# Rounding a weight block from the upper word's digits while the lower word is still being added

## The chip, the cores and the metric

The kernel runs on one core of a Trainium2 chip. The time is the device time of one execution in microseconds (us), and the figure quoted for a kernel is the median of its runs. Beside the runs there is one profiled execution, whose trace gives the start, the duration and the waits of every instruction on the engines: PE (matrix products) with PEld (its weight loads), DVE (vector), ACT (scalar), POOL (GpSimd) and SP (which issues DMAs).

## The reference, cut to what matters

Attention in hash buckets over q, k and v (2 batches, 8 heads, 768 positions, 64 wide) gives x with 1536 rows of 512. Two dense layers follow, the first with a gate, the second with a leaky slope:

```python
g = x @ w_gate
silu = g * (1.0 / (1.0 + np.exp(-g)))
x = silu * (x @ w_val) @ w_out            # d_ff 1536
h = x @ w_in
g = np.maximum(h, 0.0) + alpha * np.minimum(h, 0.0)
return g @ w_out                          # d_ff 2048
```

The attention's inputs are float32. The weights reach the chip as 64-bit floating-point numbers, in blocks of 128 x 512, and are turned into float32 there.

## The kernel before, in words

**Precision.** PE takes operands in a shortened float32 form. Every operand is therefore a pair: a high half `h`, which is the number rounded to that form, and a low half `l`, which is the number less `h`. `mm3` (line 608) multiplies a weight pair by an activation pair in three matmuls, in this order: high by high (line 611), high by low (612), low by high (613). So the third matmul of each group is the first that needs the low half.

**Order of the work.** The attention is one long row of steps (`attention`), which computes scores, takes the greatest of each row, subtracts, takes the exponential and multiplies by v. The first dense layer works on groups of 256 rows of x: `stage1(g)` for g = 0 to 3 as soon as the attention has finished that group's rows, with further attention steps between its own (`RATES` says how many), and `stage1w` on 512 columns for the rest. `stage2` is the second layer, three times 512 columns. The order in which the instructions stand on each engine within `stage1` is set by a scheduler that works from the dependencies and its own estimates; a few instructions are pinned to the order in which they are written (`pin`), among them those of `w_early` and of all of `stage1w` and `stage2`. Each engine then works off its row in order, and an instruction that waits holds up all that stand behind it.

**A new weight block.** The first layer has 36 blocks. Each is made once, while `stage1(0)` uses it; the pair is then written to memory (`w_put`) and later groups load it from there. The second layer's 32 blocks are made by `w_early` (12, during groups 2 and 3) and `w_late` (20, during `stage1w`). A block of 64-bit numbers arrives in `raw64` (two buffers). `round64` makes float32 of it, in integers:

1. ACT, line 509: the lower word, scaled, gives in `wr` the digits that the upper word lacks, rounded.
2. DVE, lines 510 and 512: shifts and masks of the upper word give sign, exponent and leading digits in `wt`.
3. POOL, line 514: the integer sum of the two, written over `wt`.

Then the pair is made in `wb`:

4. ACT, line 549 (`w_h`): `wt` rounded, the high half.
5. POOL or DVE in turn, line 556 (`w_l`): `wt` less the high half, the low half. Of the 36 blocks of the first layer POOL does the even ones and DVE the odd ones (`PL`).

`w_ahead` runs these steps a few blocks ahead of the block in use (`LEAD`). `wt` has three buffers, `wr` two, `wb` five; `WB` holds the first and the last of these.

Of the kernel before, what the change touches and what calls it, by code (L numbers as in the profile page):

```python
# [8 lines left out]
F32 = mybir.dt.float32  # L9
F32R = mybir.dt.float32r  # L10
I32 = mybir.dt.int32
U32 = mybir.dt.uint32
AF = mybir.ActivationFunctionType
ALU = mybir.AluOpType
# [9 lines left out]
WB = (3, 5)  # L24
# [22 lines left out]
def lsh_attention_moe_kernel(  # L47
# [12 lines left out]
    nc = tc.nc  # L60
# [4 lines left out]
    P = 128  # L65
# [15 lines left out]
    def f32(ap):  # L81
        return ap.bitcast(F32)
# [390 lines left out]
    NWT = len(seq)  # L473
    fresh = [w not in seq[:i] for i, w in enumerate(seq)]
    new = [n or w >= F2I for n, w in zip(fresh, seq)]
    raw, wt, ready = {}, {}, {}
    ws = Bag()
    ws.pin = True
    ws.load = ws.conv = ws.h = ws.l = ws.used = ws.put = 0
# [5 lines left out]
    def pin(ins):  # L485

        if ws.pin:
            tc.keep_in_program_order(ins)

    def raw_load(w):  # L490
        t = wp.tile([P, 512, 2], I32, tag="raw64", name="raw64", bufs=RAWB)
        pin(nc.sync.dma_start(out=t, in_=wblk[w].bitcast(I32).rearrange("p (f t) -> p f t", t=2)))
        return t
# [9 lines left out]
        elif w < F2I:  # L503
            nc.sync.dma_start(out=f32(w_tile(i)), in_=scratch[w])

    def round64(t, a):

        r = wp.tile([P, 512], I32, tag="wr", name="wr", bufs=2)
        pin(nc.scalar.activation(out=r, in_=t.bitcast(U32)[:, :, 0], func=AF.Copy, scale=float(2.0 ** -29)))
        pin(nc.vector.tensor_scalar(out=a, in0=t[:, :, 1], scalar1=3, scalar2=0x3FFFFFF8,  # L510
                                    op0=ALU.logical_shift_left, op1=ALU.bitwise_and))
        nc.vector.scalar_tensor_tensor(out=a, in0=t[:, :, 1], scalar=-0x40000000, in1=a,  # L512
                                       op0=ALU.bitwise_and, op1=ALU.bitwise_or)
        pin(nc.gpsimd.tensor_tensor(out=a, in0=a, in1=r, op=ALU.add))  # L514

    def w_conv(i):
        w = seq[i]
        if w >= F2I:
            wt[i] = fin.w[:, w - F2I, :]
        elif fresh[i]:  # L520
            wt[i] = wp.tile([P, 512], F32, tag="wt", name="wt", bufs=WB[0])
        if i in raw:
            round64(raw.pop(i), wt[i].bitcast(I32))

    def w_late():

        rs = []
        for w in late + [None] * RAWB:
            if len(rs) == RAWB or w is None:
                r, v = rs.pop(0)  # L530
                round64(r, fin.w[:, v - F2I, :].bitcast(I32))
            if w is not None:
                rs.append((raw_load(w), w))
            yield

    def w_early():

        for w in early:
            r = raw_load(w)
            yield  # L540
            t = wp.tile([P, 512], F32, tag="wt", name="wt", bufs=WB[0])
            round64(r, t.bitcast(I32))
            yield
            nc.sync.dma_start(out=whole[w - F2I], in_=t)
            yield
# [5 lines left out]
    def w_l(i):  # L551

        if new[i]:
            n, m = PL
            eng = nc.gpsimd if i % n < m else nc.vector
            eng.tensor_tensor(out=ready[i][:, 1, :], in0=wt.pop(i), in1=f32(ready[i])[:, 0, :], op=ALU.subtract)  # L556

    def w_put(i):
        if fresh[i] and seq[i] < F2I:
# [8 lines left out]
    def w_ahead(n):  # L568

        for name, k, fn in (("load", 2, w_load), ("conv", 1, w_conv), ("h", 0, w_h)):  # L570
            upto(name, n + LEAD[0] + k, fn)
        upto("l", n + LEAD[0], w_l)
        upto("h", n + LEAD[1], w_h)
        upto("put", n + 1, w_put)
        upto("conv", n + LEAD[2], w_conv)
        while ws.load < min(NWT, n + (LEAD[3] if fresh[min(ws.load, NWT - 1)] else LEAD[2])):
            upto("load", ws.load + 1, w_load)
# [176 lines left out]
    wp = ctx.enter_context(tc.tile_pool(name="wp", bufs=1))  # L754
# [27 lines left out]
    def prime(k):  # L782

        if k == 60:
            setup_alpha()
        k -= PRIME[0]
        if k >= 0 and k % PRIME[1] == 0:
            i = k // PRIME[1]
            upto("load", min(i, 7), w_load)
            if i >= 4:  # L790
                upto("conv", min(i - 3, 4), w_conv)
# [7 lines left out]
    at.alone = False  # L799
    at.tag = dict(S="SSM", m="S", hp="S", po="po")  # L800
    early_steps = w_early()
    ws.pin = False
    for g, rate in enumerate(RATES):
# [77 lines left out]
```

## Time and profile before

| | us |
|---|---|
| median of 3 runs (912.88 to 914.37) | 914.33 |
| the profiled execution | 911.48 |
| its span, first to last instruction | 909.7 |
| PE busy in the span | 840.9 (92%) |
| DVE busy | 576.1 (63%) |
| ACT busy | 440.4 (48%) |
| POOL busy | 378.2 (42%) |
| mean granted clock of PE, as a share of the full one | 0.981 |

A busy share is a mean over stages with different limits, so the stages are read one by one. Up to about 60 us the attention runs alone; from there to about 240 us the first layer's blocks are made and used; from about 240 to 560 us groups 1 to 3 run beside the rest of the attention; then `stage1w`, and from about 640 us `stage2`. "Busy" includes time in which an instruction has begun and is held up by something other than a semaphore.

### The profile page before, as it was taken

How to read it: one execution, taken by the hardware profiler on the slowest of the kernel's cores; microseconds unless marked ns; L12 is line 12 of the kernel's file. 1: busy time of each engine (PE TensorE's matmuls, PEld its weight loads, DVE VectorE, ACT ScalarE, POOL GpSimd, SP SyncE). 2: the span in 40 equal slices, each digit the busy share in tenths (PEclk: the TensorE clock that was granted, in tenths of full speed). 3: DMA queues.
4: the chain of work that ended last, by engine and by line, in shares of the span. 5: the costliest groups of instructions: out<-in, count | busy, mean ns of one | idle time of the engine just before them, and what ended most of it. 6: DMA issues, size and time to landing. Idle time of an engine off the chain costs nothing.

```text
span 909.7 us, 13016 instructions
## 1 busy us (share of the span) xinstructions
PE 840.9 (92%) x4816; PEld 734.1 (81%) x4816; DVE 576.1 (63%) x856; ACT 440.4 (48%) x760; POOL 378.2 (42%) x327
## 2 busy tenths in 40 slices
PE   4797788777899999999999999999999999999998
PEld 3576677666798999999999987788888888888886
DVE  5599999988766657677777537663543353435432
ACT  5687566646555565656565323222433343333331
POOL 4214665766533212232222225543444445435442
PEclk8899989999999999999999999999999999999999
DMA  9424676979999756767766698887200010001001
GB/s 219 102 76 160 215 255 220 261 223 268 306 323 293 218 177 232 250 217 229 261 204 219 219 342 295 331 334 267 105 1 1 1 48 0 1 9 39 1 0 47
DMA packets 63487, 158.45 MB, mean 174 GB/s; under 512 B 18112, under 2 KB 24256, under 8 KB 63424
## 3 DMA queue, kind: packets, MB, share of 16 engines
q1 hardware_dynamic: 61264, 152.07, 50.7%
q0 software_dynamic: 2016, 5.51, 2.9%
q8 instruction: 38, 0.62, 0.3%
q14 instruction: 25, 0.20, 0.1%
q10 hardware_dynamic: 144, 0.05, 0.0%
HBM read 132.44 MB, written 25.17 MB: 173 GB/s over the span
## 4 chain that ended last, share of the span: by engine, by line
PE 68%; DVE 14%; POOL 3%; ACT 3%; DMA 3%; issue 2%; SPq 0%; POOLq 0%; DVEq 0%; ACTq 0%
PE po L319 8%; PE gp L611 6%; PE gp L613 5%; PE gp L612 5%; PE op L618 5%; PE hp L613 5%; PE op L617 5%; PE hp L612 5%; PE hp L611 5%; PE op L616 5%; PE yp L613 3%; PE yp L611 3%; PE yp L612 3%; DVE wt L510 2%; DMA wb<-w 2%
## 5 line engine op out<-in xcount | busy, mean ns | idle before, releaser
L606 POOL TENSOR_TENSOR gl<-ex,gh 128x512 fp32r<-128x512 f32 (+1 forms) x108 | 118.3, 1095 | 213.4 <-ACT gh L603 157.7
L611 PE MATMUL gp<-xh,wb 128*128 128x256 f32 (+1 forms) x480 | 156.4, 326 | 10.5 <-ACT wb L549 5.4
L613 PE MATMUL gp<-xh,wb 128*128 128x256 f32 (+1 forms) x480 | 151.1, 315 | 9.7 <-POOL wb L556 6.6
L612 PE MATMUL gp<-xl,wb 128*128 128x256 f32 (+1 forms) x480 | 149.5, 312 | 2.6 <-POOL xl L348 2.6
L319 PE MATMUL po<-se,vv 128*128 128x256 f32 x576 | 143.2, 385 | 9.1 <-DVE xf L341 3.4
L319 PEld LDWEIGHTS po<-se,vv 128*128 128x128 f32 x576 | 103.8, 193 | 22.3 <-ACT se L312 5.0
L549 ACT ACTIVATE wb<-w 128x512 fp32r<-128x512 f32 x96 | 60.7, 632 | 117.8 <-PE hp L613 79.1
L611 PEld LDWEIGHTS gp<-xh,wb 128*128 128x128 f32 x480 | 93.9, 196 | 21.0 <-ACT wb L549 9.0
L603 ACT ACTIVATE gh<-ex 128x512 fp32r<-128x512 f32 (+1 forms) x108 | 57.8, 535 | 105.2 <-DVE ex L600 46.7
L556 POOL TENSOR_TENSOR wb<-w,wb 128x512 fp32r<-128x512 f32 x48 | 62.1, 1294 | 110.3 <-ACT wb L549 106.2
L613 PEld LDWEIGHTS gp<-xh,wb 128*128 128x128 f32 x480 | 94.4, 197 | 15.8 <-POOL wb L556 7.6
L612 PEld LDWEIGHTS gp<-xl,wb 128*128 128x128 f32 x480 | 94.3, 196 | 7.0 <-POOL xl L348 2.8
L312 ACT ACTIVATE se<-se 128x1536 f32<-128x1536 f32 x48 | 71.3, 1485 | 50.5 <-DVE se L307 50.3
L556 DVE TENSOR_TENSOR wb<-w,wb 128x512 fp32r<-128x512 f32 x48 | 36.4, 758 | 91.2 <-ACT wb L549 91.2
L307 DVE SCALAR_TENSOR_TENSOR se<-se,mb 128x1536 f32<-128x1536 f32 x48 | 83.7, 1744 | 8.3 <-PE mb L302 8.0
L282 ACT ACTIVATE se<-S 128x512 f32<-128x512 f32 x144 | 80.1, 593 | 16.9 <-PE S L281 15.6
L514 POOL TENSOR_TENSOR wt<-wt,wr 128x512 int32<-128x512 int32 x48 | 68.2, 1421 | 47.3 <-DVE wt L512 33.7
L280 PE MATMUL S<-QA,kt 128*128 128x256 f32 x288 | 80.3, 308 | 1.6 <-ACT se L282 1.4
L611 PE MATMUL yp<-gh,wb 128*128 128x256 f32 (+1 forms) x240 | 76.2, 319 | 5.4 <-ACT wb L549 3.8
L613 PE MATMUL yp<-gh,wb 128*128 128x256 f32 (+1 forms) x240 | 72.9, 310 | 6.4 <-POOL wb L556 4.3
L281 PE MATMUL S<-qb,kt 76*128 76x256 f32 x288 | 73.5, 286 | 1.4 <-ACT kt L203 1.2
L611 PE MATMUL hp<-xh,wb 128*128 128x512 f32 x192 | 74.7, 389 | 0.0
(94 smaller groups left out, 1848.4 us busy)
## 6 DMA issues: line engine op xcount, KB each, us to landing
wb<-w SPq DMA_DIRECT2D x144, 512.0 KB, 4.4
raw<-in_wblk_dram SPq DMA_DIRECT2D x68, 512.0 KB, 4.3
w<-wb SPq DMA_DIRECT2D x36, 512.0 KB, 5.0
qr<-in_q_dram SPq DMA_DIRECT2D x24, 256.0 KB, 3.7
kt<-in_k_dram POOLq DMA_DIRECT2D x14, 384.0 KB, 8.1
nat<-in_k_dram SPq DMA_DIRECT2D x8, 384.0 KB, 5.2
vv<-in_v_dram SPq DMA_DIRECT2D x16, 192.0 KB, 6.8
whole<-wt SPq DMA_DIRECT2D x12, 256.0 KB, 2.2
```

The costliest lines, as they stand in the source:

```text
L280: nc.tensor.matmul(pt[:, i, :], lhsT=ka[:, sl], rhs=qa, start=True, stop=False)
L281: nc.tensor.matmul(pt[:, i, :], lhsT=kb[:, sl], rhs=qb, start=False, stop=True)
L282: nc.scalar.activation(out=u.se[:, 2 * j:2 * j + 2, :], in_=pt, func=AF.Copy)
L307: nc.vector.scalar_tensor_tensor(out=u.se, in0=u.se, scalar=FLOOR, in1=u.mx[:, None, :].to_broadcast([P, NC, GQ]), op0=ALU.max, op1=ALU.su ...
L312: nc.scalar.activation(out=u.se, in_=u.se, func=AF.Exp, scale=SCALE)
L319: nc.tensor.matmul(it.po[:, u.x, :], lhsT=VV[it.b, it.p][:, kb, u.x * D:u.x * D + P], rhs=u.se[:, kb, :], start=kb == 0, stop=kb == NC - 1)
L514: pin(nc.gpsimd.tensor_tensor(out=a, in0=a, in1=r, op=ALU.add))
L556: eng.tensor_tensor(out=ready[i][:, 1, :], in0=wt.pop(i), in1=f32(ready[i])[:, 0, :], op=ALU.subtract)
L606: nc.gpsimd.tensor_tensor(out=l, in0=ex, in1=f32(h), op=ALU.subtract)
L611: nc.tensor.matmul(pt, lhsT=h, rhs=ah, start=first, stop=False)
L612: nc.tensor.matmul(pt, lhsT=h, rhs=al_, start=False, stop=False)
L613: nc.tensor.matmul(pt, lhsT=l, rhs=ah, start=False, stop=last)
```

## The change

The POOL addition of a first-layer block (line 514) writes its sum into `wr`, and no longer over `wt`. `wt` keeps the upper word's digits alone. The high half (step 4) is the rounding of those digits, so that it needs DVE's line 512 and no longer POOL's line 514. The low half (step 5) is the sum, from `wr`, less the high half; so the pair still adds up to the same number. Step 5 now waits for the addition and for the rounding, which may run side by side. `wr` gets three buffers and `wt` two. The blocks of the second layer are made as before, with the new buffer counts.

```diff
-    def round64(t, a):
+    def round64(t, a, apart=False):
...
-        r = wp.tile([P, 512], I32, tag="wr", name="wr", bufs=2)
+        r = wp.tile([P, 512], I32, tag="wr", name="wr", bufs=WB[0])
...
-        pin(nc.gpsimd.tensor_tensor(out=a, in0=a, in1=r, op=ALU.add))
+        if apart:
+            pin(nc.gpsimd.tensor_tensor(out=r, in0=a, in1=r, op=ALU.add))
+        else:
+            pin(nc.gpsimd.tensor_tensor(out=a, in0=a, in1=r, op=ALU.add))
+        return r
...
-            wt[i] = wp.tile([P, 512], F32, tag="wt", name="wt", bufs=WB[0])
+            wt[i] = wp.tile([P, 512], F32, tag="wt", name="wt", bufs=2)
         if i in raw:
-            round64(raw.pop(i), wt[i].bitcast(I32))
+            whl[i] = round64(raw.pop(i), wt[i].bitcast(I32), apart=True).bitcast(F32)
...
-            t = wp.tile([P, 512], F32, tag="wt", name="wt", bufs=WB[0])
+            t = wp.tile([P, 512], F32, tag="wt", name="wt", bufs=2)
...
-            eng.tensor_tensor(out=ready[i][:, 1, :], in0=wt.pop(i), in1=f32(ready[i])[:, 0, :], op=ALU.subtract)
+            w = wt.pop(i)
+            w = whl.pop(i) if i in whl else w
+            eng.tensor_tensor(out=ready[i][:, 1, :], in0=w, in1=f32(ready[i])[:, 0, :], op=ALU.subtract)
```

In the changed kernel the addition of line 514 is line 515 for these blocks, line 549 is 553, and from line 556, which is 562, all numbers are six higher.

The dependencies being others, the scheduler also sets the instructions in another order, from the first blocks of `stage1(0)` to the end of the attention. Two places on DVE show it. In the names, the number behind a tile tells one block's buffer from another's; a block's `wr` has the number after its `wt`. The first place is the last block but two of `stage1(0)`, `wt_2080`, whose subtraction gives `wb_2111`. Before:

```order
L510 TENSOR_SCALAR wt_2080<-raw64_1994 128x512
L594 SCALAR_TENSOR_TENSOR ex_2132<-ex_2132,gp_2088 128x256
L512 SCALAR_TENSOR_TENSOR wt_2080<-raw64_1994,wt_2080 128x512
L297 TENSOR_REDUCE mq_2350<-mt_2347 128x2
L307 SCALAR_TENSOR_TENSOR se_2016<-se_2016,mb_2369 128x1536
L510 TENSOR_SCALAR wt_2114<-raw64_2039 128x512
L556 TENSOR_TENSOR wb_2111<-wt_2080,wb_2111 128x512
```

Now:

```order
L510 TENSOR_SCALAR wt_2080<-raw64_1994 128x512
L600 SCALAR_TENSOR_TENSOR ex_2132<-ex_2132,gp_2088 128x256
L512 SCALAR_TENSOR_TENSOR wt_2080<-raw64_1994,wt_2080 128x512
L562 TENSOR_TENSOR wb_2111<-wr_2081,wb_2111 128x512
L286 TENSOR_TENSOR m2_2472<-se_2296 128x512
```

Three instructions stood between the block's line 512 and its subtraction; now none does. Over the 18 blocks that DVE subtracts, 77 rows stood between the two, and 64 do now.

The second place is the last block of `stage1(0)`, `wt_2160`, whose subtraction gives `wb_2194`. Before:

```order
L335 STREAM_TRANSPOSE xf_2407<-den_2404 128x256
L289 TENSOR_TENSOR m1_2475<-m2_2472 128x256
L510 TENSOR_SCALAR wt_2160<-raw64_2086 128x512
L336 RECIPROCAL r8_2408<-xf_2407 128x8
L512 SCALAR_TENSOR_TENSOR wt_2160<-raw64_2086,wt_2160 128x512
L337 STREAM_TRANSPOSE den_2404<-r8_2408 128x256
L341 TENSOR_TENSOR xf_2407<-po_2254,den_2404 64x256 x2
L286 TENSOR_TENSOR m2_2586<-se_2416 128x512
L556 TENSOR_TENSOR wb_2194<-wt_2160,wb_2194 128x512
```

Now:

```order
L289 TENSOR_TENSOR m1_2475<-m2_2472 128x256
L510 TENSOR_SCALAR wt_2160<-raw64_2086 128x512
L512 SCALAR_TENSOR_TENSOR wt_2160<-raw64_2086,wt_2160 128x512
L307 SCALAR_TENSOR_TENSOR se_2016<-se_2016,mb_2369 128x1536
L562 TENSOR_TENSOR wb_2194<-wr_2161,wb_2194 128x512
L335 STREAM_TRANSPOSE xf_2407<-den_2404 128x256
L336 RECIPROCAL r8_2408<-xf_2407 128x8
L337 STREAM_TRANSPOSE den_2404<-r8_2408 128x256
L341 TENSOR_TENSOR xf_2407<-po_2254,den_2404 64x256 x2
```

The attention's output step (lines 335 to 341) and one line 286 stood ahead of the last subtraction and now stand behind it; all else that DVE did up to that point it still does up to that point.

## Rows read from the trace of the kernel before

**Rows 1.** Busy time by stretch: the stretch, its length, each engine's busy us
```profile
76.00:242.00 166.00, 128.80 (x796) 111.52 (x795) 156.47 (x213) 101.18 (x181) 106.46 (x86) 0.95 0.77 243
242.00:560.00 318.00, 311.86 (x2222) 294.91 (x2221) 209.84 (x350) 170.21 (x304) 90.24 (x89) 1.00 0.76 249
560.00:909.70 349.70, 344.40 (x1514) 284.17 (x1512) 156.84 (x205) 117.43 (x189) 159.29 (x122) 1.00 0.23 83
```
**Rows 2.** Waits of PE, 76 to 242 us: us in total, times, longest
```profile
PE gp L613 <- POOL wb L556: 6.6, 5, 3.1
PE gp L611 <- ACT wb L549: 5.4, 9, 1.1
PE yp L613 <- POOL wb L556: 4.3, 5, 1.2
PE yp L611 <- ACT wb L549: 3.8, 8, 0.9
PE gp L613 <- DVE wb L556: 3.0, 2, 2.5
...
PE yp L613 <- DVE wb L556: 2.1, 1, 2.1
```
**Rows 3.** Waits of the other engines, 76 to 242 us
```profile
POOL wb L556 <- ACT wb L549: 10.6, 11, 2.6
...
DVE ex L591 <- ACT ex L588: 2.7, 2, 2.3
...
DVE wb L556 <- ACT wb L549: 2.6, 3, 1.8
```
**Rows 4.** Chain of waits, 76 to 242 us, shares by line
```profile
by line: DVE wt L510 11.3%; POOL wt L514 10.7%; DVE wt L512 10.4%; issue 9.6%; DVE se L307 5.9%; DVE wb L556 5.3%; POOL wb L556 5.2%; DVE m L287 4.6%; ACT wb L549 4.3%; DVE m L289 3.9%; DVE m L286 2.7%; DVE xf L341 1.9%; POOL gl L606 1.8%; 
```
**Rows 5.** Groups of instructions, 76 to 242 us: busy us, mean ns | idle before
```profile
L512 DVE SCALAR_TENSOR_TENSOR wt<-raw,wt 128x512 int32<-128x512 int32 x35 | 34.0, 971 | 0.1
L510 DVE TENSOR_SCALAR wt<-raw 128x512 int32<-128x512 int32 x35 | 27.3, 779 | 0.1
...
L556 DVE TENSOR_TENSOR wb<-wt,wb 128x512 fp32r<-128x512 f32 x18 | 17.0, 947 | 3.2 <-ACT wb L549 2.6
...
L514 POOL TENSOR_TENSOR wt<-wt,wr 128x512 int32<-128x512 int32 x35 | 50.0, 1429 | 32.7 <-DVE wt L512 27.8 <-ACT wb L549 2.8 <-ACT wr L509 1.4
L556 POOL TENSOR_TENSOR wb<-wt,wb 128x512 fp32r<-128x512 f32 x18 | 25.0, 1387 | 11.3 <-ACT wb L549 10.6 <-DMA w<-wb 0.7
...
L549 ACT ACTIVATE wb<-wt 128x512 fp32r<-128x512 f32 x36 | 22.6, 628 | 33.8 <-POOL wt L514 33.8
```
**Rows 6.** Lines 510 and 512 alone, 76 to 242 us: ns min/median/max, first and last start
```profile
L510 DVE TENSOR_SCALAR wt<-raw x35: 379/428/2340, 75.8 to 234.0; 128x512 int32<-128x512 int32 x35
...
L512 DVE SCALAR_TENSOR_TENSOR wt<-raw,wt x35: 644/687/2311, 76.6 to 235.0; 128x512 int32<-128x512 int32 x35
```
**Rows 7.** Timeline of POOL and DVE, 136 to 172 us: start, us, instruction, idle before
```profile
158.52 1.29 POOL L514 TENSOR_TENSOR wt<-wt,wr 128x512 int32<-128x512 int32 x1 [1.89 <-DVE wt L512]
159.76 1.19 POOL L606 TENSOR_TENSOR gl<-ex,gh 128x256 fp32r<-128x256 f32 x1
...
168.74 1.58 POOL L556 TENSOR_TENSOR wb<-wt,wb 128x512 fp32r<-128x512 f32 x1 [0.74 <-ACT wb L549]
...
158.63 1.72 DVE L287 SCALAR_TENSOR_TENSOR m<-se,m 128x512 f32<-128x512 f32 x1
```
**Rows 8.** Timeline of DVE, 224 to 242 us, end of the last new block
```profile
233.10 0.45 DVE L335 STREAM_TRANSPOSE xf<-den 128x256 f32<-128x256 f32 x1 [0.61 <-ACT den L325]
...
236.59 0.43 DVE L337 STREAM_TRANSPOSE den<-r 128x256 f32<-128x256 f32 x1
237.13 0.86 DVE L341 TENSOR_TENSOR xf<-po,den 64x256 f32<-64x256 f32 x2
238.02 0.69 DVE L286 TENSOR_TENSOR m<-se 128x512 f32<-128x512 f32 x1
```
**Rows 9.** Timeline of DVE, 182 to 196 us, one subtraction
```profile
193.51 0.69 DVE L556 TENSOR_TENSOR wb<-wt,wb 128x512 fp32r<-128x512 f32 x1 [1.83 <-ACT wb L549]
```

More of the change, by code (lines that the diff above doesn't have):

```diff
@@ L475, in lsh_attention_moe_kernel @@
     new = [n or w >= F2I for n, w in zip(fresh, seq)]
-    raw, wt, ready = {}, {}, {}
+    raw, wt, whl, ready = {}, {}, {}, {}
     ws = Bag()
```

## The prediction

> **What bounds the kernel now.** I read the busy times by stretch first [rows 1]. From 242 us to the end PE is busy for 311.86 of 318 us and for 344.40 of 349.70 us: both stretches are bound by PE, and the change leaves PE's matmuls as they are. From 76 to 242 us PE is busy for only 128.80 of 166 us, and DVE for 156.47. Since later work is PE work in a row, a microsecond by which this stretch gets shorter should arrive whole at the end, so the stretch is the place to look.
>
> Next, what PE waits for there [rows 2]. The six rows with `wb` are waits for a block's high half (5.4 and 3.8 us) or low half (6.6, 4.3, 3.0 and 2.1 us): 25.2 of PE's 37.2 us of idle time. So PE waits for new weights. The chain of waits shows what they wait for [rows 4]: it runs through DVE's lines 510 and 512, POOL's additions (10.7%), and ACT's rounding of the high half, line 549, with 4.3%, which is 7.1 us of 166. So the rounding that the change takes from between two other steps does lie on the path, though it is a small part of it.
>
> The third view is what the makers do. DVE's idle time is 166 less 156.47, or 9.5 us. Yet it is not at its own speed for the rest: lines 510 and 512 have medians of 428 and 687 ns [rows 6] but means of 779 and 971 ns [rows 5]. The 35 of each take 27.3 and 34.0 us where at the median they would take 15.0 and 24.0, so 22.3 us are something else. The timeline shows what [rows 7]: POOL's addition at 158.52 lasts until 159.81; DVE's line 287, begun at 158.63, takes 1.72 us and ends at 160.35, 0.54 us after the addition; POOL's next instruction, begun at 159.76, takes 1.19 us and ends at 160.95, 0.60 us after line 287. I read them as one after the other: each held the other off for a whole instruction, and the one that waited went next.
>
> **The change part by part.** *The high half no longer waits for the addition.* Line 549 takes 628 ns [rows 5] and before it the block waits for POOL's 1429 ns. PE gets the high half sooner by about that addition, but this alone is worth little: `mm3` needs the low half at its third matmul, so PE goes on by two matmuls and stands there.
>
> *The low half no longer waits for the rounding, only for the later of the two.* Where POOL does addition and subtraction, it idled 0.74 us between them [rows 7]; POOL's waits of this kind are 11 and 10.6 us in all [rows 3]. The path gains at most the 7.1 us of line 549 in the chain and some 0.11 us of hand-over at each of the 11 places: 8.3 us. At least it gains nothing, for DVE is busy for 94% of the stretch, and when one wait goes, DVE's next instruction is the next thing that is late. Between 0 and 8.3 us I look at DVE, the busiest engine: 2.6 us of its idle time ended on line 549 directly, and 2.7 us on a chain that went through PE's gate matmuls, which had waited for weights [rows 3]. Of these 5.3 us I take half, 2.6 us, since DVE's subtraction was also moved nearer to its own line 512, which spends part of the shorter wait.
>
> *DVE's order.* The attention's output step and one line 286 stood ahead of the last subtraction of the stage and now stand behind it. In the trace those are 0.45, 0.43, 0.86 and 0.69 us [rows 8], 2.4 us, without the short reciprocal. They move from a stretch in which DVE is late to one in which DVE is busy for 209.84 of 318 us [rows 1], where PE's work covers them. If the cover failed, they would cost the same 2.4 us again; I count the gain whole: 2.4 us. The lower bound is 0, if PE had then to wait for that attention output.
>
> *What costs nothing.* The addition and the subtraction read and write as many elements as before, in the same numbers (35 and 36 in the stretch), so POOL, DVE and ACT do the same work. No DMA is added. `wt` loses a buffer: new blocks come 4.65 us apart (35 starts of line 510 from 75.8 to 234.0 us, [rows 6]), so two buffers are 9.3 us, and the digits are done with after line 512, the addition and the rounding, 687 + 1429 + 628 ns or 2.7 us when each goes at once. `wr` must now last until the subtraction, and has three buffers, 14 us. The blocks that `w_early` makes fall into the stretch from 242 us on, where PE has 6.1 us of idle time in 318; none of it can be laid to them, and I give nothing for their buffer. ACT, which now has line 549 earlier in its row, is busy for 101.18 of 166 us; a wait on it would hold up its exponentials, but line 549 waits for less than before.
>
> *The sum.* 2.6 + 2.4 = 5.0 us off the profiled execution's 911.48 us. The median of the runs lies 2.85 us above that execution, and I take the difference as it is: 914.3 - 5.0 = **909.3 us**. For this case alone, from 0.2% up to both terms at their upper ends (8.3 + 2.4 us), the range is 903.6 to 912.5 us.
>
> **A rule against the change.** The row shows first that DVE and POOL held each other off for whole instructions [rows 7]. The Trainium skill, "SBUF — State Buffer", section "Who interferes with whom", says that DVE and GpSimd share a pair of ports under an exclusive lock, taken for a whole instruction, by DVE instructions with two SBUF inputs among others. The trace agrees. By that rule packing POOL's two instructions closer together would win nothing once the lock is always held. That is the first rival, and its size comes from rows.
>
> **The rivals.** *Nothing moves, because the two engines already share all of the time.* POOL is busy for 106.46 us [rows 1]. The three lines of DVE that make weights would, undisturbed, take 15.0 + 24.0 us and 18 times 0.69 us [rows 9], or 12.4: 51.4 us. The sum is 157.9 of 166 us, and the attention's two-input steps are not yet in it, though some of POOL's busy time is itself waiting and counted twice. For it: 22.3 us of DVE's time went into such waits. Against it: DVE still has 9.5 us of true idle time, and waits for `wb` end PE's idle time 30 times. A second way to the same result is that the rounding, though free of the addition, comes no sooner, since ACT's row puts it behind an exponential. Time: 914.3 us, less or more by 1.8.
>
> *More than forecast: DVE loses all its idle time.* Then 9.5 + 2.4 = 11.9 us go: 902.4 us. For it: PE's 25.2 us of waits for weights would allow it. Against it: of DVE's 9.5 us only 5.3 have to do with weights at all.
>
> *Slower: DVE parks behind POOL.* DVE's subtraction now stands nearer to its own line 512: 64 rows between the two where 77 stood, and none for the third block from the end. DVE works in order. If POOL is busy when line 512 ends, the addition comes after that instruction, and DVE stands still for it with the attention's steps behind it. One such stop costs a POOL instruction more, 1.43 us [rows 5]. The trace has one of this kind already, 1.83 us [rows 9]. With the gain eaten up by the closer order, two new stops of 18 (2.9 us) make the kernel slower by over 0.2%, and three give 4.3 us: 918.6 us. For it: the scheduler's estimates do not show that the two engines hold each other off. Against it: a DVE instruction with two inputs would often have stood there for POOL anyway.
>
> **How the numbers follow.** A measurement of this kernel tells about 0.2%, 1.8 us, from no change. Forecast 909.3 us: 45%. All idle time gone, 902.4 us: 12%. Nothing moves: 19%. DVE parks: 24%. So faster by over 0.2%: 0.57; within: 0.19; slower: 0.24. The range goes from 903.6 us, which leaves out part of the greatest gain, to 918.6 us, which leaves out more than three stops: together less than 2 in 10.
>
> **What would show it.** Right: in the stretch of new blocks POOL's wait for line 549 (10.6 us) nearly gone and its subtraction close behind the addition; PE's waits for the high half (9.2 us) mostly gone, those for the low half (16.0 us) smaller; the last subtraction 4 to 6 us earlier, and PE as busy after that as before. For the first rival: the same rows moved, but DVE's lines 510, 512 and 287 longer, and the last subtraction at the same time. For the last one: DVE's subtraction with much idle time before it, ended by POOL's addition. The forecast is wrong if the last subtraction is no earlier, or if it is and PE then idles between 242 and 560 us for more than 6.1 us.

## The result, and the profile of the changed kernel

| | before | changed |
|---|---|---|
| median of 7 runs each (lowest, highest) | 913.13 us (911.29, 914.37) | 919.75 us (915.79, 923.16) |
| the profiled execution | 911.48 | 921.85 |
| its span | 909.7 | 920.1 |
| mean granted clock of PE | 0.981 | 0.972 |

The ratio of the times is 1.007, with a 95% interval from 1.0047 to 1.0093: **slower by 0.7%, or 6.6 us**. The forecast was 909.3 us with a range that ended at 918.6.

The first view is again the busy time by stretch; it answers to [rows 1].

```profile
76.00:242.00 166.00, 126.83 (x764) 111.58 (x763) 146.26 (x202) 96.90 (x173) 103.94 (x83) 0.91 0.74 238
242.00:560.00 318.00, 310.56 (x2225) 294.94 (x2224) 209.79 (x353) 172.42 (x307) 85.73 (x88) 0.99 0.74 243
560.00:910.00 350.00, 344.85 (x1517) 284.02 (x1516) 161.57 (x211) 118.58 (x191) 164.90 (x127) 1.00 0.25 88
```

The loss lies in the stretch of new blocks and in the first 20 us behind it; in the rest PE is as busy as before. In the first row DVE was idle for 9.53 us and now is for 19.74, and it began 202 instructions where it had begun 213. PE's idle time grew by only 2.0 us there. The stretch from 130 to 242 us alone, before and then changed, shows what else grew:

```profile
130.00:242.00 112.00, 86.01 (x541) 73.96 (x540) 102.79 (x142) 67.40 (x121) 73.83 (x60) 0.97 0.83 256
```
```profile
130.00:242.00 112.00, 86.02 (x496) 76.40 (x496) 92.76 (x131) 62.19 (x111) 69.31 (x57) 0.86 0.78 245
```

PE is busy for the same 86 us and begins 45 matmuls fewer, at a mean granted clock of 0.86 in place of 0.97. So PE spent more of this time at the lower of its two clock levels, and much of the loss shows as slower matmuls and not as idle time. No run here takes the waits and the clock apart.

The waits of the same stretch answer to [rows 2, 3] (total us, times, longest); PE's are first.

```profile
PE gp L619 <- POOL wb L562: 11.7, 7, 3.5
PE yp L619 <- POOL wb L562: 6.8, 4, 2.6
PE gp L619 <- DVE wb L562: 4.1, 4, 1.5
...
PE yp L617 <- ACT wb L553: 3.6, 2, 2.1
PE gp L617 <- ACT wb L553: 2.5, 3, 1.3
...
PE yp L619 <- DVE wb L562: 1.1, 2, 0.7
```
```profile
DVE wb L562 <- POOL wr L515: 8.6, 5, 4.3
DVE se L307 <- PE mb L302: 4.8, 2, 2.5
```

PE's waits for the high half fell from 9.2 us (5.4 and 3.8) to 6.1; those for the low half rose from 16.0 to 23.7. POOL's subtraction no longer waits for the rounding in any row of this view, where it had waited for 10.6 us. In its place stands a row that was not there: DVE's subtraction waits five times for POOL's addition, 8.6 us in all. DVE's line 307 also waits longer for PE, 4.8 us where it was 0.4. By lines (busy us, mean ns, idle before) DVE's subtraction answers to its row in [rows 5]:

```profile
L562 DVE TENSOR_TENSOR wb<-wr,wb 128x512 fp32r<-128x512 f32 x17 | 20.0, 1179 | 8.6 <-POOL wr L515 8.6
```

A subtraction of DVE took 947 ns on the mean and now takes 1179, beside the waits. The longest stop, in the timeline of POOL and of DVE:

```profile
187.94 1.28 POOL L612 TENSOR_TENSOR gl<-ex,gh 128x256 fp32r<-128x256 f32 x1 [2.44 <-ACT gh L609]
189.30 1.90 POOL L175 TENSOR_TENSOR kt<-nat,kt 64x768 fp32r<-64x768 f32 x1
191.28 2.48 POOL L515 TENSOR_TENSOR wr<-wt,wr 128x512 int32<-128x512 int32 x2
193.72 1.25 POOL L562 TENSOR_TENSOR wb<-wr,wb 128x512 fp32r<-128x512 f32 x1
...
188.88 0.63 DVE L289 TENSOR_TENSOR m<-m 128x256 f32<-128x256 f32 x1
193.79 1.73 DVE L562 TENSOR_TENSOR wb<-wr,wb 128x512 fp32r<-128x512 f32 x1 [4.29 <-POOL wr L515]
```

DVE's part of the block, line 512, had ended at 187.7 us. POOL stood until 187.94 for a gate's high half, did that gate's subtraction and the keys' subtraction (line 175), and only then the two additions. DVE's next instruction needed the second one, so DVE did nothing for 4.29 us, and then its subtraction met POOL's, begun 0.07 us earlier, and lasted 1.73 us.

The end of the stretch holds a second loss. DVE and SP there:

```profile
240.67 1.75 DVE L307 SCALAR_TENSOR_TENSOR se<-se,mb 128x1536 f32<-128x1536 f32 x1 [2.54 <-PE mb L302]
242.34 0.68 DVE L562 TENSOR_TENSOR wb<-wr,wb 128x512 fp32r<-128x512 f32 x1
...
245.76 0.32 SPq L504 DMA_DIRECT2D wb<-w  x1
246.18 0.38 SPq L566 DMA_DIRECT2D w<-wb  x1
```

The last subtraction, and the store of its pair, in the kernel before:

```profile
238.79 0.69 DVE L556 TENSOR_TENSOR wb<-wt,wb 128x512 fp32r<-128x512 f32 x1
...
239.51 0.32 SPq L560 DMA_DIRECT2D w<-wb  x1
```

SP's waits from 240 to 246 us, and the chain of waits behind the store (start, us, what):

```profile
SPq L504 <- PE S L281: 5.8, 1, 5.8
```
```profile
247.08 13.06 DMA wb<-w
...
260.28 0.55 PE gp L617
260.83 0.21 PE gp L618
...
265.25 0.12 PE gp L618
```

The last subtraction began at 242.34 us, 3.6 us later than before. Right ahead of it in DVE's row now stands line 307, which waited 2.54 us for PE and took 1.75. The subtraction ended at 243.02, but the store of its pair (line 566) left only at 246.18: ahead of it in SP's row stands a load for the next group, which had waited 5.8 us. In the kernel before, the store left at 239.51, just after the subtraction. Behind the store come further loads; the weights that PE stood for landed at 260.14. PE's matmuls then came 0.21 us apart, and 0.12 only from 265 us on.

### The profile page after: what moved, and what is told of

Its sections match the earlier page's. It is cut to its first block, busy times and chain, and to the rows that moved or that the text cites. A ratio compares the mean times of both kernels' runs of the same rounds, so it can differ in the third digit from the quotient of the medians.

```text
span 920.1 us, 13041 instructions
## 1 busy us (share of the span) xinstructions
PE 844.7 (92%) x4816; PEld 739.2 (80%) x4816; DVE 572.0 (62%) x856; ACT 440.8 (48%) x760; POOL 376.8 (41%) x327
## 4 chain that ended last, share of the span: by engine, by line
PE 65%; DMA 4%; DVE 4%; ACT 1%; POOL 1%; issue 1%; SPq 0%; DVEq 0%; POOLq 0%; ACTq 0%
PE po L319 8%; PE gp L617 5%; PE gp L618 5%; PE gp L619 5%; PE op L622 5%; PE hp L617 5%; PE hp L618 5%; PE op L623 5%; PE op L624 5%; PE hp L619 5%; DMA wb<-w 3%; PE yp L619 3%; PE yp L617 3%; PE yp L618 2%; PE S L280 2%; PE S L281 2%
## 5 line engine op out<-in xcount | busy, mean ns | idle before, releaser
L319 PE MATMUL po<-se,vv 128*128 128x256 f32 x576 | 146.9, 390 | 5.6 <-ACT se L312 2.6
L617 PE MATMUL yp<-gh,wb 128*128 128x256 f32 (+1 forms) x240 | 77.8, 325 | 5.4 <-ACT wb L553 3.6
L619 PE MATMUL yp<-gh,wb 128*128 128x256 f32 (+1 forms) x240 | 73.3, 311 | 7.9 <-POOL wb L562 6.8
L617 PE MATMUL hp<-xh,wb 128*128 128x512 f32 x192 | 74.7, 389 | 0.0
L618 PE MATMUL hp<-xl,wb 128*128 128x512 f32 x192 | 74.7, 389 | 0.0
L619 PE MATMUL hp<-xh,wb 128*128 128x512 f32 x192 | 74.7, 389 | 0.0
```

Of the source, the lines that this page charges most:

```text
L319: nc.tensor.matmul(it.po[:, u.x, :], lhsT=VV[it.b, it.p][:, kb, u.x * D:u.x * D + P], rhs=u.se[:, kb, :], start=kb == 0, stop=kb == NC - 1)
L617: nc.tensor.matmul(pt, lhsT=h, rhs=ah, start=first, stop=False)
L618: nc.tensor.matmul(pt, lhsT=h, rhs=al_, start=False, stop=False)
L619: nc.tensor.matmul(pt, lhsT=l, rhs=ah, start=False, stop=last)
```

## The experiments

The change does two things: it alters what waits for what, and it lets the scheduler set the rows anew. To take them apart, rows were held: each instruction gets an edge, without a semaphore, to the one that stands before it in a row written down beforehand (the lines below give this in outline). "Old order" is the row of every engine and of SP's queue in the kernel before, "new order" that of the changed kernel; both kernels issue the same instructions. All ratios are to the kernel before, with 95% intervals.

```diff
         stage2(n * W)
+    for e in engines:
+        for a, b in zip(row[e], row[e][1:]):
+            tc.add_manual_dep(ins[e][b], ins[e][a].name, NO_SYNC, reason="order")
```

### Split or order

**The change in the old order** (`row` is that of the kernel before).

> The changed kernel (digits and sum apart, same buffers), but every engine's row and SP's queue are held to the order of the kernel before. Theory 'order': the change lost its time because the scheduler set the rows anew, and the split itself is harmless; then 909 to 914 us, most likely 912, since the rounding of the high half keeps its old, late place in ACT's row and can use little of its freedom; DVE's waits for POOL's addition before a subtraction stay as before (1.8 us in all). Rival 'split': the split itself, or wt with two buffers, costs the time; then 918 to 922 us as the changed kernel.

Measured: 908.09 us, ratio 0.9933 (0.9913 to 0.9954): faster than both kernels, and than either expectation.

**The kernel before in the new order.**

> The kernel before (digits and sum in one tile, its own buffers), but every engine's row and SP's queue are held to the order of the changed kernel. Theory 'order': 919 us or more, up to 930, since ACT's rounding now stands early in its row and yet has to wait for POOL's addition. Rival 'split': the order is harmless, 911 to 915 us.

Measured: 928.46 us, ratio 1.0154 (1.0134 to 1.0175).

**The change with the old buffers.**

```diff
-        r = wp.tile([P, 512], I32, tag="wr", name="wr", bufs=WB[0])
+        r = wp.tile([P, 512], I32, tag="wr", name="wr", bufs=2)
...
-            wt[i] = wp.tile([P, 512], F32, tag="wt", name="wt", bufs=2)
+            wt[i] = wp.tile([P, 512], F32, tag="wt", name="wt", bufs=WB[0])
```

> The change without its buffers: digits and sum apart, but wt keeps three buffers and wr two, and the scheduler is free. It sets every row and SP's queue exactly as in the changed kernel, so this is the new order with the old buffers. Theory 'order': 918 to 922 us. Rival 'two buffers of wt hold the digits up in the new, bunched order': 912 to 916 us.

Measured: 920.94 us, ratio 1.0095 (1.0077 to 1.0114). Its interval overlaps the change's own, so in the new order the buffers cost nothing that shows, and the split alone makes the scheduler set that order.

| ratio to before | old order | new order |
|---|---|---|
| sum written over the digits | 1 | 1.0154 |
| sum apart | 0.9933 | 1.007 (old buffers 1.0095) |

So the split, with its buffers, gains 0.7% (6.1 us) in the old order, and without them 0.6% (1.0154 less 1.0095, 5.4 us) in the new one; the new order costs 1.4 to 1.5% (12.5 to 14 us) with either. Busy time of 76 to 242 us in the first two:

```profile
76.00:242.00 166.00, 132.38 (x837) 117.10 (x836) 158.14 (x217) 104.24 (x185) 107.54 (x87) 0.94 0.78 252
```
```profile
76.00:242.00 166.00, 125.38 (x721) 108.39 (x720) 138.38 (x194) 92.98 (x165) 97.01 (x78) 0.88 0.69 218
```

With the split in the old order DVE idles for 7.86 us and PE begins 837 matmuls; with the old dependency in the new order DVE idles for 27.62 us and PE begins 721. The waits of the split in the old order show the gain:

```profile
PE gp L619 <- POOL wb L562: 7.9, 5, 3.4
PE gp L619 <- DVE wb L562: 5.2, 4, 2.8
PE yp L619 <- POOL wb L562: 4.5, 4, 1.2
...
PE yp L619 <- DVE wb L562: 1.2, 2, 0.8
...
PE yp L617 <- ACT wb L553: 0.9, 1, 0.9
...
PE gp L617 <- ACT wb L553: 0.8, 1, 0.8
```
```profile
POOL wb L562 <- ACT wb L553: 4.5, 3, 2.7
```

The high half's 9.2 us are down to 1.7, at 18.8 us for the low half where it was 16.0, and DVE does not wait for POOL's additions at all. POOL's waits for the rounding, 10.6 us before, are down to 4.5. The last subtraction comes 5.9 us earlier than in the kernel before:

```profile
232.87 0.68 DVE L562 TENSOR_TENSOR wb<-wr,wb 128x512 fp32r<-128x512 f32 x1
```

### Where in time

Five kernels with the sum apart, each with one order up to a cut and the other behind it (`row[e] = new[e][:cut[e]] + old[e][cut[e]:]` and the like).

**New order up to 187 us.**

> The changed kernel with its own order up to about 187 us (SP 75, PE 820, DVE 238, ACT 212, POOL 87 instructions), and from there the order of the kernel before. Up to there the changed kernel was 1.7 us ahead in its trace. Theory 'the rows behind 187 us lost the time' (DVE stops before a subtraction, first loads of the next group): 911 to 914 us. Rival 'the loss is laid earlier, by the buffers or the place of the k loads on POOL's queue at 177 us': 916 to 920 us.

Measured: 921.39 us, ratio 1.0085 (1.0064 to 1.0107).

**New order from 187 us on.**

> The changed kernel with the order of the kernel before up to about 187 us and its own order from there (the complement of the run that had its own order first, 921.4 us). Theory 'the loss is laid by what stands before 187 us': 908 to 911 us, as with the old order throughout. Rival 'each half of the new order costs its part': 913 to 917 us.

Measured: 912.33 us, ratio 0.9998 (0.9979 to 1.0017).

**New order up to 130 us.**

> The changed kernel with its own order up to about 130 us and the old order from there. Theory 'the new order loses between 130 and 187 us': 907 to 911 us, as with the old order throughout. Rival 'the part before 130 us lays the loss': 917 to 921 us.

Measured: 909.81 us, ratio 0.9959 (0.9942 to 0.9975).

**New order from 130 to 187 us.**

> The changed kernel with the old order up to about 130 us and from 187 us on, and its own order in between. Theory 'the new order loses between 130 and 187 us': 919 to 922 us, as with its own order up to 187 us. Rival 'the part before 130 us lays the loss': 908 to 912 us.

Measured: 929.16 us, ratio 1.0163 (1.014 to 1.0187): slower than the change itself, and outside both expectations.

**New order up to 240 us.**

> The changed kernel with its own order up to about 240 us (SP 102, PE 1107, DVE 303, ACT 268, POOL 111 instructions), and from there the order of the kernel before. Theory 'half of the loss arises at the start of the next group, by the order there': the last 5 us stay away, 914 to 916 us. Rival 'that is only what a late end of the first group makes of its loads and of the clock': 918 to 921 us, as the changed kernel.

Measured: 928.12 us, ratio 1.0147 (1.0117 to 1.0177): again slower than the change itself, and outside both expectations.

Ahead of 130 us the new order does little harm. Behind 187 us alone it costs 0.65% over the old order, so "nothing but what stands before 187 us" is refuted as well. The parts do not add up: a cut has a price of its own. In the run with the new order from 130 to 187 us, DVE was busy for only 10.60 of the 20 us behind the first cut:

```profile
130.00:150.00 20.00, 13.99 (x68) 12.20 (x67) 10.60 (x13) 6.72 (x11) 9.62 (x8) 0.74 0.43 152
```

So these runs say that the cost arises from 130 us on, on both sides of 187, and no more.

### Mending the new order

**Additions first**, on POOL's row:

```diff
+wr  L515 addition
 gl  L612 gate subtraction
-wr  L515 addition
...
+wr  L515 addition
+wr  L515 addition
 gl  L612 gate subtraction
 kt  L175 keys' subtraction
-wr  L515 addition
-wr  L515 addition
 wb  L562 weight subtraction
```

> The changed kernel in its own order, but at two places of POOL's row the additions of new blocks go first: one addition ahead of the gate subtraction at 171.01 us, two ahead of the gate subtraction at 187.94 us and the keys' subtraction at 189.30 us. DVE stood there for 1.57 and 4.29 us for an addition. Theory 'DVE parks behind POOL': both stops go, about 5 us of DVE's time, and the kernel comes to 914 to 917 us. Rival 'the order as a whole puts attention late, and DVE's stops only show it': less than 1.5 us gained, 918 to 921 us.

Measured: 920.93 us, ratio 1.0089 (1.0067 to 1.0112): no gain. Busy time and DVE's waits of that kernel, 76 to 242 us:

```profile
76.00:242.00 166.00, 129.02 (x755) 114.80 (x753) 151.21 (x201) 96.01 (x170) 103.54 (x81) 0.88 0.74 239
```
```profile
DVE se L307 <- PE mb L302: 4.7, 3, 3.2
DVE wb L562 <- POOL wr L515: 2.8, 3, 1.5
```

DVE's stops for POOL fell from 8.6 to 2.8 us, and its busy time rose by 5 us with one instruction fewer: that time went into instructions that last longer. Behind the longest stop the subtraction began 3.3 us earlier, at 190.53 us, but the last one of the stretch began at 242.36, as late as in the changed kernel. DVE's next instruction, the keys' subtraction (line 175), shows where time went: begun while POOL did its own line 175, it took 2.44 us where it had taken 0.95.

```profile
191.77 2.44 DVE L175 TENSOR_TENSOR kt<-nat,kt 64x768 fp32r<-64x768 f32 x1
```

This is the prediction's reading of [rows 7], an instruction held off by the other engine. The Trainium skill, "SBUF — State Buffer", section "Who interferes with whom", says that a DVE instruction with two SBUF inputs contends with a GpSimd instruction that reads SBUF. This trace agrees, in the 2.44 us. Longer instructions alone do not make the kernel slow, though: over the whole run DVE was busy for 572.0 us in the changed kernel, for 580.3 in this one, and for 578.5 in the split with the old order, the fastest of all.

**The keys' load later**, `L164` behind two additions and a subtraction on POOL's row.

> The changed kernel in its own order, but on POOL's row the first load of keys (issued at 176.84 us after POOL had waited 3.87 us for a score matmul) stands three instructions later, behind two additions and a subtraction. Theory 'POOL's row is held by that load': the two additions come up to 3.9 us sooner, and 1.5 to 4 us arrive at the end: 916 to 918 us. Rival 'it is covered, DVE being at other work there': 919 to 921 us.

Measured: 920.35 us, ratio 1.0088 (1.0065 to 1.0111): nothing gained.

**Both.**

> Both edits of POOL's row together. Theory 'the stops between POOL and DVE are the loss': 910 to 914 us, near the 908.1 us of the changed kernel in the old order. Rival 'the order as a whole': 917 us or more, no better than the first edit alone.

Measured: 923.23 us, ratio 1.0106 (1.0083 to 1.0129): no better.

**Attention earlier on PE**, by 10 places.

> The changed kernel in its own order, but in PE's row the attention's hash matmuls and transposes (lines 191, 192, 295, 302) stand 10 matmuls earlier between 147 and 226 us. Theory 'attention behind weights': the new order put these short matmuls behind gate and output matmuls that wait for a low half (the pair on line 295 began at 160.76 us in the changed kernel with the old order and at 168.06 and 170.32 us with the new one), so exponentials come late and DVE runs out of work; moved back in part, 913 to 917 us. Rival 'PE's row alone does not matter, DVE's and ACT's rows are as late': 918 to 921 us.

Measured: 926.72 us, ratio 1.014 (1.0117 to 1.0163): slower. In that trace PE's line 295 stands twice for ACT's copy of the scores, 6.6 us from 76 to 242 us, with weight matmuls behind it; the changed kernel had 0.2 us of such waits. Attention earlier on PE's row, at least by these 10 places, does not mend it; the time is outside both expectations.

**DVE's subtractions later**, by three places.

> The changed kernel in its own order, but each of DVE's subtractions of new blocks between 136 and 249 us stands about three DVE instructions later in DVE's row. Theory 'DVE parks behind POOL': DVE does the attention's steps first and finds the sum made, most of its 8.6 us of waits for POOL's additions go, 913 to 917 us. Rival 'DVE and POOL hold each other off whatever the order': the waits go but come back inside DVE's instructions, 918 to 922 us, and DVE's summed durations grow by what its idle time loses.

Measured: 933.57 us, ratio 1.0229 (1.0211 to 1.0248): the slowest of all, outside both expectations. PE's waits:

```profile
PE gp L619 <- DVE wb L562: 17.6, 7, 3.9
...
PE yp L619 <- DVE wb L562: 8.7, 4, 4.6
```

DVE's low half made PE wait for 26.3 us instead of 5.2. Its place in DVE's row is urgent: to fill the stop in front of it with three other instructions cost more than the stop.

**SP's queue in the old order.**

> The changed kernel in its own order on the engines, but SP's queue of transfers stands in the old order. Theory 'the first loads of the next group are late because of the new queue order': the 4.7 us that the trace lost between 248 and 261 us go, 914 to 917 us. Rival 'they are late because the last blocks are': 918 to 921 us.

Measured: 917.09 us, ratio 1.0047 (1.0024 to 1.0069). PE, 242 to 262 us, in the changed kernel and in this one:

```profile
242.00:262.00 20.00, 16.11 (x112) 14.80 (x111) 12.26 (x23) 10.55 (x19) 5.05 (x6) 0.90 0.87 230
```
```profile
242.00:262.00 20.00, 19.60 (x150) 18.68 (x149) 13.19 (x23) 11.29 (x21) 5.69 (x7) 1.00 1.02 307
```

The gap at the start of the next group is gone in this trace, 38 matmuls more in 20 us. In the medians it is worth some 2 us, with intervals that overlap the change's: likely, not shown.

### Which engine's row

All with the sum apart and the old order, except where said.

**POOL's row and SP's queue new.**

> The changed kernel with POOL's row and SP's queue in the new order, and PE, DVE and ACT in the old one. Theory 'the loss is in how PE, DVE and ACT interleave attention and weights': 907 to 912 us, as with the old order throughout (908.1). Rival 'POOL's and SP's rows carry it': 914 to 919 us.

Measured: 918.74 us, ratio 1.009 (1.0054 to 1.0126).

**POOL's row alone new.**

> The changed kernel with POOL's row alone in the new order, all else in the old one. Theory 'PE, DVE and ACT': 907 to 911 us. Rival 'POOL's row': 913 us or more. Its difference from the run with POOL's row and SP's queue in the new order is the price of the queue in the old order of the engines; in the new order of the engines it was 2 to 3 us.

Measured: 919.91 us, ratio 1.0082 (1.0057 to 1.0107). So 39 moved instructions of POOL, at 13 places, put into the old order of all else, cost 1.5% (1.0082 less 0.9933), as much as the new order as a whole. SP's queue makes no difference here. As with the cuts in time, such a mixture can have a price of its own. The reverse, POOL's old row in the new order of all else, was not run, so this does not show that POOL's row is what costs the time in the changed kernel.

**Five of the 39 new**, on POOL's row:

```diff
-kt  L175 keys' subtraction
-wr  L515 addition
-wb  L562 weight subtraction
 gl  L612 gate subtraction
+kt  L175 keys' subtraction
+wr  L515 addition
 wr  L515 addition
+wb  L562 weight subtraction
```

> The changed kernel in the old order, but five neighbouring POOL instructions at about 182 to 190 us stand as in the new order: gate subtraction, keys' subtraction, addition, addition, weight subtraction, where the old order has keys, addition, weight subtraction, gate, addition. In the changed kernel and in the run with POOL's new row DVE stood there for 4.29 and 4.25 us for the second addition. Theory 'this place of POOL's row parks DVE, with attention and weights behind it': 911 to 915 us, 3 to 7 us above the old order's 908.1. Rival 'the two orders only clash in sum, no place carries it': 907 to 910 us.

Measured: 912.3 us, ratio 0.9993 (0.9974 to 1.0012), 0.6% (5.5 us) above the old order throughout.

**The other 34 new.**

> The complement: the changed kernel in the old order with POOL's row in the new order at all its other 12 places (34 instructions). Theory 'the place of the five carries half or more of POOL's 11.8 us': 910 to 915 us. Rival 'the other places carry it': 916 to 920 us.

Measured: 914.32 us, ratio 1.0006 (0.9987 to 1.0026), 0.73% (6.7 us) above it. Together 1.33% of POOL's 1.5%.

One place of five instructions thus holds two fifths of this loss, as the two parts measured. POOL's, DVE's and PE's timelines with the five moved:

```profile
184.90 1.41 POOL L612 TENSOR_TENSOR gl<-ex,gh 128x256 fp32r<-128x256 f32 x1 [4.48 <-ACT gh L609]
186.39 1.79 POOL L175 TENSOR_TENSOR kt<-nat,kt 64x768 fp32r<-64x768 f32 x1
188.26 2.48 POOL L515 TENSOR_TENSOR wr<-wt,wr 128x512 int32<-128x512 int32 x2
...
196.70 1.29 POOL L515 TENSOR_TENSOR wr<-wt,wr 128x512 int32<-128x512 int32 x1 [4.74 <-ACT wr L509]
```
```profile
190.77 1.73 DVE L562 TENSOR_TENSOR wb<-wr,wb 128x512 fp32r<-128x512 f32 x1 [5.04 <-POOL wr L515]
...
197.14 1.40 DVE L286 TENSOR_TENSOR m<-se 128x512 f32<-128x512 f32 x1 [3.57 <-ACT se L282]
```
```profile
192.01 0.58 PE L619 MATMUL gp<-xh,wb 128*128 128x256 f32 x1 [7.41 <-POOL wb L562]
```

And 180 to 200 us there, then with the old order throughout:

```profile
180.00:200.00 20.00, 12.04 (x67) 10.90 (x65) 10.67 (x17) 6.92 (x13) 9.82 (x8) 0.77 0.47 155
```
```profile
180.00:200.00 20.00, 15.62 (x106) 13.73 (x106) 19.63 (x25) 10.72 (x21) 13.09 (x11) 0.98 0.72 236
```

It is the stop of the changed kernel: POOL waits for a gate, and DVE for POOL, 5.04 us. But DVE is not the only one: PE waits 7.41 us for POOL's subtraction, which stands behind the same two additions. PE's next matmuls then come 0.21 us apart; the granted clock of these 20 us is 0.77 against 0.98. ACT's copy of the scores waits 10.13 us for PE, with line 509 behind it in ACT's row. So it comes back: POOL waits 4.74 us for ACT's line 509, and DVE 3.57 us for the copy. In 20 us DVE loses 9 us of work, and 5.5 arrive at the end. Which part DVE's stop has in that, and which PE's, no run tells apart.

## Why the prediction was wrong, point by point

- **What bounds the kernel:** right as to the place. Nearly all of the difference arises between 76 and 262 us, and in each later stretch PE is as busy as before. That PE's clock in this stretch would fall with its waits (0.97 to 0.86) was in none of the terms.
- **High half free of the addition:** right in part. PE's waits for it fell by a third, and those for the low half rose by more. In the old order 7.5 of its 9.2 us went. What it is worth alone no run shows.
- **Low half waits for the later of two:** taken at 2.6 us between 0 and 8.3. The direction was right: in the old order POOL waited less for the rounding and the last subtraction came 5.9 us earlier. The term was too small: the split as a whole, with the high half, measured 0.67% (0.46 to 0.87%), some 6.1 us there, and 5.4 us in the new order. How that divides between the two halves no run shows.
- **DVE's order:** this is the step that failed. The prediction counted two steps that moved behind the last subtraction as a gain of 2.4 us, and put the rest of the new order at nothing in the sum. The new order costs 12.5 to 14 us, over twice what the split gains. The output step did move, yet the last subtraction began 3.6 us later: line 307 now stands ahead of it and waited 2.54 us for PE. POOL's row was not priced, and its 39 moved instructions, put into the old order, are enough to cost 1.5%. SP's row was not priced either.
- **Buffers at nothing:** agrees in the new order, within the intervals.
- **POOL, DVE and ACT do the same work:** right. Over the whole run DVE was busy for 572.0 us where it had been for 576.1, POOL for 376.8 against 378.2, and ACT for 440.8 against 440.4. DVE's subtraction alone got longer, 1179 ns in place of 947.
- **The rival "nothing moves":** its mechanism shows in the run with the additions first, where idle time became longer instructions. As the result of the change it was wrong.
- **The rival "DVE parks behind POOL":** right in sign, and DVE did stand behind POOL's additions as it said, at 24%. That these stops are the cause is not shown: to take two of them out of the new order gave nothing. Its price was wrong as well. A stop was taken at one POOL instruction, 1.43 us; the longest took 4.29 us, because what stood ahead on POOL was itself waiting for a gate. The example it took from [rows 9], 1.83 us, was a wait for ACT's rounding and not for POOL. The five instructions alone cost 5.5 us, through DVE's stop and PE's together, which takes nearly all of the gain.
- **The range** ended at three cheap stops, 918.6 us, and did not hold 919.75. It left out the next group's loads: in the trace PE begins 38 matmuls fewer in 20 us where they come late, some 5 us of its work, and in the medians SP's old order is worth some 2 us.

What stays open: how the 34 other moves on POOL share their 6.7 us, why the new order as a whole costs what it does, of which POOL's row, SP's row and PE's clock are the parts that these runs point at, and which joint change of the rows would mend it.

## What to carry to other kernels

Where a scheduler sets the rows, an edit of a dependency is two changes, and the second can be the larger: hold the old rows and time the edit alone before judging it. Compare the rows of every engine, those off the critical path too. The price of a stop is not one instruction of the other engine but all that stands ahead there, with the waits of that as well, and every engine that needs what stands behind it. Count the matmuls that PE begins and read its granted clock, beside its waits.

## What the runs showed of the hardware

Idle time of DVE that ends on POOL can be taken away without any gain: with the additions first, 5.8 us of such waits less, 5.0 us more in DVE's instructions, and the last subtraction at the same time. And a gap on PE costs after its end too: after PE had waited for the next group's weights its matmuls came 0.21 us apart for 5 us, near twice the 0.12 of full clock, so at the lower of its two levels (1.2 GHz); the granted clock of 242 to 262 us was 0.90 on the mean, against 1.00 where the loads came in time.
